# v through GpSimd's casting queue and two PE transposes, and w2 in 384 columns, in a linear-attention and soft-MoE kernel

## The chip, the cores and the metric

The kernel runs on one core of one Trainium2 chip. The metric is the time of one execution on the device, in microseconds. The kernel before took 122.52 us, the median of three runs (122.45 to 122.78). The engines are named as in the profile: PE (matrix multiply; PEld is its weight load), DVE (VectorE), ACT (ScalarE), POOL (GpSimd) and SP (a queue that only issues transfers). SP, ACT and POOL issue the transfers (DMAs), which 16 DMA engines carry out.

## What is computed

First a linear attention (RWKV-5): for each of 4 batches and 8 heads a state of 48 x 48 runs over 768 tokens. Then a soft mixture of experts over the resulting 3,072 tokens of 384 values: each of 32 slots is a weighted mean over all tokens, eight experts (two matrices each) handle four slots each, and every token takes a weighted mean of the slots.

```python
for t in range(S):                      # attention; B, H, S, D = 4, 8, 768, 48
    kt, vt, rt = (k[:, :, t], v[:, :, t], r[:, :, t])
    cur = np.einsum('bhd,bhe->bhde', u[None] * kt, vt)
    y[:, :, t] = np.einsum('bhd,bhde->bhe', rt, state + cur)
    state = w[None, :, :, None] * state + np.einsum('bhd,bhe->bhde', kt, vt)
...
logits = x @ phi                        # MoE; x is y as 3072 x 384, phi 384 x 32
slot_input = softmax(logits, 0).T @ x
for e in range(E):                      # 8 experts; w1 384 x 1024, w2 1024 x 384
    h = np.maximum(slot_input[e] @ w1[e], 0.0)
    slot_out[e] = h @ w2[e]
return softmax(logits, 1) @ slot_out
```

(The two softmax lines stand for their few lines of exp and division.)

## The kernel before

**Tiling.** Heads are worked on in pairs, so there are 16 units (4 batches x 4 pairs, index m), and each unit is cut into two halves of three 128-token chunks. That gives 32 iterations, i = 0 to 31, of the one loop at L494; it starts at i = -5 to fill the pipeline. In it mu = i // 2 and odd = i % 2. The order of the instructions on each engine is the order in which the program writes them.

**Inputs.** k, r and v of a batch lie in one of three buffers raw0 to raw2 (batch 3 takes raw0 again, once batch 0's has been used). A partition holds six consecutive tokens of k and r for each head (runs of 1,152 bytes), and three consecutive tokens of each half for v (runs of 576 bytes). SP issues all of these loads (L115, L119): batches 0 and 1 by pairs of heads, batch 2 whole, batch 3 at i = 3 (L552).

**One unit.** `scale` (L228, POOL, for unit 0 DVE) multiplies k and r by powers of the decay w and writes bf16 into kr. POOL does this three units ahead for k and two for r, one instruction an iteration. `t_pe` (L235) transposes on PE, `t_evac` (L241, ACT) copies the result to kT or rT and puts the tokens in order. `b_pe` and `b_evac` (L247, L252) transpose kT back by chunk to kn. For v, `v_cast` (L270, ACT; unit 0 on POOL, L268) makes bf16, and `v_pe` (L284) puts the tokens in order: for each chunk three matmuls with shifted columns of a selection matrix Q3 gather the three tokens of a partition into PSUM bank Vb, nine matmuls of 96 columns a half. `v_evac` (L290, ACT) copies them to vn. Then `a_pe` (L299) and `mask_f` (L304, DVE) form the masked scores, `m_pe` and `z_evac` (L325, L341, L342) the states, `y_pe` and `y_evac` (L352 to L372) the output.

**Start.** Before the loop DVE and ACT make the tables of decay powers W (`tt`, `ex`, L188, L192), from ln w, which `spread` (L177) broadcasts over the partitions with a ones matmul; the rest of the tables follow in the first iterations (T_AT). PE runs matmuls without use (`keep_warm`, L144) until there is work.

**Weights.** POOL issues the loads of w1 and w2 (L135, L138), which cast f32 to bf16 on the way, 768 KB written for each of 16 matrices. They stand in POOL's order at iterations 13 to 26 (W_AT, L465), one behind that iteration's scaling, up to five at i = 26, and the last w2 in three pieces after the loop (rows 0-4, 4-6 and 6-8 of eight, L576). Ahead of the first stands `guard` (L571), a copy of one column that waits until k of batch 3 has landed. w1 has its own buffer; w2 goes into raw1 and raw2 once batches 1 and 2 have been used. No more than eight of POOL's loads are outstanding: each waits for the eighth before it.

**After the loop** come the last routing steps, w1 (L623), the transposes of the hidden values (L648), w2 (`second`, L660; each row of four or fewer experts in two halves of 192 columns, into banks Xb and Yb), the scaling to so (L671, L672) and the output, 24 blocks of 128 tokens (`emit`, L684 to L688), stored by SP and POOL (L704).

Of the kernel before, what the change touches and what calls it, by code (L numbers as in the profile page):

```python
# [9 lines left out]
def kernel(  # L10
# [13 lines left out]
    B, H, S, D = r.shape  # L24
    C = 128
# [26 lines left out]
    def O(ins):  # L52
        return tc.keep_in_program_order(ins)
# [11 lines left out]
    EG = E // 2  # L65
    raw = [big.tile([128, 3 * RW], f32, name=f"raw{j}") for j in range(NR)]
    eW2 = nF * Dm
# [6 lines left out]
    def raw_of(which, b):  # L74
        return raw[b % NR][:, which * RW:(which + 1) * RW]

    T0 = psb.tile([128, 1024], bf, name="T0")
# [26 lines left out]
    O(dve.memset(wu[:], 1.0))  # L104
    O(sp.dma_start(out=w_row, in_=w.rearrange("(o h) d -> o (h d)", o=1)))
    O(act.preload_act_table_set("natural_log_exp_and_others"))
    O(act.dma_start(out=wu3[0:4, :, 0:D], in_=w.rearrange("(q e) d -> q e d", e=2)))
    O(act.dma_start(out=wu3[4:8, :, 0:D], in_=u.rearrange("(q e) d -> q e d", e=2)))
    O(dve.memset(warm, 0.0))
    O(dve.memset(one_f, 1.0))  # L110
    zt = cst.tile([128, nQ, 3, P2], f32, name="zt")
    O(dve.memset(zt[:], 0.0))

    def load_kr(which, src, b, h0, h1):
        O(sp.dma_start(out=raw_of(which, b).rearrange("p (h x) -> p h x", h=H)[:, h0:h1, :],  # L115
                       in_=src[b, h0:h1].rearrange("h (p j) d -> p h (j d)", j=J)))

    def load_v(b, h0, h1):
        O(sp.dma_start(out=raw_of(2, b).rearrange("p (h x) -> p h x", h=H * G)[:, h0 * G:h1 * G, :],  # L119
                       in_=v[b, h0:h1].rearrange("h (g p j) d -> p (h g) (j d)", g=G, j=JV)))  # L120

    def load_batch(b, step):
        for h0 in range(0, H, step):
            load_kr(0, k, b, h0, h0 + step)
            load_kr(1, r, b, h0, h0 + step)
            load_v(b, h0, h0 + step)

# [13 lines left out]
    def keep_warm(n, bank=Yb, data=None):  # L141
        data = warm if data is None else data
        for _ in range(n):
# [7 lines left out]
                         pattern=[[-1, 128]], channel_multiplier=1))  # L151
    QW = 2 * C + JV - 1 + C
    Q3 = cst.tile([128, QW], bf, name="Q3")
    O(pool.memset(Q3[:], 0.0))
    O(pool.affine_select(out=Q3[:], in_=Q3[:], compare_op=ALU.not_equal, fill=1.0, base=JV - 1,
                         pattern=[[-1, QW]], channel_multiplier=JV))
    mask_ut = cst.tile([128, 128], f32, name="mask_ut")
# [37 lines left out]
    tt(1, 0)  # L195
    spread(Vb, P2, H * D)
    ex(0, 0)
# [3 lines left out]
    def wu_steps(n):  # L201
# [5 lines left out]
        if n == 1:  # L207
            O(dve.tensor_mul(ucol[0:64, :, 0], wuT[0:64, 0:4], wuT[0:64, 4:8]))
            O(dve.tensor_mul(ucol[64:128, :, 1], wuT[64:128, 0:4], wuT[64:128, 4:8]))

    O(pool.memset(zt[0:64, :, :, 0:D], 1.0))
    O(pool.memset(zt[64:128, :, :, D:P2], 1.0))
    ones = cst.tile([128, 128], bf, name="ones")
    Le_t = [cst.tile([128, L, 128], bf, name=f"Le{j}") for j in range(2)]
    phi_s = cst.tile([128, nM, ES], bf, name="phi_s")
    phi_b = cst.tile([128, nM * ES], bf, name="phi_b")
    assert JV == nM
    acc = cst.tile([128, NA], f32, name="acc")
    guard = cst.tile([128, 1], f32, name="guard")
    st = {}  # L220
# [40 lines left out]

    def v_cast(m):
        b, q = divmod(m, nQ)
        vb = wk.tile([128, 2, G, JV, D], bf, name="v_bf", bufs=2)
        st["vb", m] = vb
        out, src = vb[:].rearrange("p h g j d -> p (h g j d)"), raw_of(2, b)[:, 2 * q * G * JV * D:2 * (q + 1) * G * JV * D]
        if m == 0:
            O(pool.tensor_copy(out, src))  # L268
        else:
            O(act.copy(out, src))  # L270


    def at(i):
        m, g = divmod(i, G)
        b, q = divmod(m, nQ)
        return m, b, q, g, b * G + g

    def v_pe(i):
        m, b, q, g, n = at(i)
        vb = st["vb", m]  # L280
        for c in range(L):
            for j in range(JV):
                o = C * c - j + JV - 1
                O(pe.matmul(Vb[:, c * P2:(c + 1) * P2], Q3[:, o:o + C], vb[:, :, g, j, :],  # L284
                            start=(j == 0), stop=(j == JV - 1)))

    def v_evac(i):
        vn = wk.tile([128, L, 2, D], bf, name="vn", bufs=3)
        st["v", i] = vn
        O(act.copy(vn[:].rearrange("p c e d -> p (c e d)"), Vb[:, 0:L * P2]))  # L290

# [145 lines left out]
    def route(i, part):  # L437
# [23 lines left out]
        if s < 2 * L:  # L461
# [4 lines left out]
    T_AT = {-4: [(tt, 0, 1), (tt, 1, 1), (ex, 0, 1), (tt, 0, 2)], -3: [(ex, 1, 1), (ex, 0, 2)],  # L466
            -1: [(tt, 1, 2), (ex, 1, 2)], 0: [(tt, 0, 3), (ex, 0, 3)], 1: [(tt, 1, 3), (ex, 1, 3)]}
    Z_AT = {-3: 0, -1: 1, 1: 2, 2: 3}
    nw = 0
# [24 lines left out]
    for i in range(-5, nH):  # L494
# [53 lines left out]
        if i == 2:  # L548
            O(pool.memset(ones[:], 1.0))
            for t in Le_t:  # L550
                O(pool.memset(t[:], 0.0))
        if i == 3:  # L552
            load_kr(0, k, B - 1, 0, H)
            load_kr(1, r, B - 1, 0, H)
            for h0 in range(0, H, 2):
                load_v(B - 1, h0, h0 + 2)
        if i == 5:
            O(act.copy(phi_b[:], phi_f))
        if i == 6:
# [10 lines left out]
        if i == min(W_AT):  # L570
            O(pool.tensor_copy(guard[:], raw_of(0, B - 1)[:, 0:1]))  # L571
# [81 lines left out]
    row_recip(0, 8)  # L653
    SO = [Xb[:, 0:HD], Yb[:, 0:HD]]

    def second(g, experts):
        for y in range(nF):
            for x in range(2):
                for j in experts:
                    O(pe.matmul(SO[x][32 * j:32 * j + 32, :], hT[g][:, y, 32 * j:32 * j + 32],  # L660
                                w2_of(g * EG + j)[:, y, x * HD:(x + 1) * HD],
                                start=(g == 0 and y == 0), stop=(g == 1 and y == nF - 1), skip_group_check=True))

# [5 lines left out]
    row_sums(8, 12)  # L669
    so = cst.tile([128, Dm], bf, name="so")  # L670
    O(dve.tensor_scalar_mul(so[:, 0:HD], SO[0], csr[:, 0:1]))  # L671
    O(act.activation(out=so[:, HD:Dm], in_=SO[1], func=AF.Copy, scale=csr[:, 0:1]))  # L672
    row_recip(8, 12)
# [3 lines left out]
    sizes = [1, 1, 2, 2, 2, 4, 4, 4, 4]  # L677
    obuf = ([raw[0][:, 16 * Dm:17 * Dm], raw[0][:, 17 * Dm:18 * Dm], Wf[0][:, 0:2 * Dm], Wf[1][:, 0:2 * Dm],
             Wf[0][:, 2 * Dm:4 * Dm]]
# [55 lines left out]
```

The softmax here doesn't subtract the row's maximum and nothing guards it: scores larger than these inputs give would overflow.

## Time and profile before

| | us |
|---|---|
| median of three runs | 122.52 |
| the profiled execution | 122.36 |
| its span, first to last instruction | 120.5 |
| busy: PE, DVE, ACT, POOL | 102.6, 96.4, 83.7, 59.7 |
| POOL's scalings, 30 x 1.426 | 42.2 |
| first issue of a weight load on POOL | 40.22 |
| last piece of w2 used by PE | 103.83 |

The span is what the trace shows from the first to the last instruction; the difference to the execution's time, 1.86 us, lies outside. A busy time is a sum of the durations of an engine's instructions; it says nothing yet of what the end waits for. The page also cuts the span into 40 slices of 3.01 us, with the busy share of each engine and of the DMA engines in tenths, and the chain of waits follows the end back through what released each step. A timeline gives one engine's instructions in order: start, duration, engine, line, operation, output and inputs, and in brackets the idle time ahead and what ended it.

### The profile page before, as it was taken

How to read it: one execution, taken by the hardware profiler on the slowest of the kernel's cores; microseconds unless marked ns; L12 is line 12 of the kernel's file. 1: busy time of each engine (PE TensorE's matmuls, PEld its weight loads, DVE VectorE, ACT ScalarE, POOL GpSimd, SP SyncE). 2: the span in 40 equal slices, each digit the busy share in tenths (PEclk: the TensorE clock that was granted, in tenths of full speed). 3: DMA queues.
4: the chain of work that ended last, by engine and by line, in shares of the span. 5: the costliest groups of instructions: out<-in, count | busy, mean ns of one | idle time of the engine just before them, and what ended most of it. 6: DMA issues, size and time to landing. Idle time of an engine off the chain costs nothing.

```text
span 120.5 us, 4334 instructions
## 1 busy us (share of the span) xinstructions
PE 102.6 (85%) x1795; PEld 82.9 (69%) x1797; DVE 96.4 (80%) x187; ACT 83.7 (69%) x183; POOL 59.7 (50%) x70
## 2 busy tenths in 40 slices
PE   5996977799999999999999999999979996796000
PEld 1465866687887988898888898888866686583000
DVE  6899999999999999899999899999943510399000
ACT  4459769797978998888898988997963510299000
POOL 7349534599999999797677593101000000012000
PEclk9999999999999999999999999999999999999755
DMA  2999999999999999999999999999999998069992
GB/s 38 322 362 373 374 367 371 364 391 362 330 380 382 323 204 216 218 213 212 220 206 222 211 220 209 215 215 215 224 208 220 208 206 165 16 261 389 396 420 100
DMA packets 20925, 31.79 MB, mean 264 GB/s; under 512 B 1129, under 2 KB 18026, under 8 KB 20906
## 3 DMA queue, kind: packets, MB, share of 16 engines
q0 software_dynamic: 2960, 14.55, 55.5%
q1 hardware_dynamic: 17922, 16.96, 41.3%
q8 instruction: 14, 0.23, 0.7%
q14 instruction: 5, 0.04, 0.1%
q10 hardware_dynamic: 24, 0.00, 0.0%
HBM read 39.38 MB, written 4.72 MB: 366 GB/s over the span
## 4 chain that ended last, share of the span: by engine, by line
PE 37%; DMA 31%; DVE 15%; issue 6%; ACT 1%; POOL 1%; POOLq 0%; DVEq 0%; ACTq 0%
DMA raw<-in_moe_w_dram 31%; PE Vb L284 5%; PE T L235 4%; PE Ab L299 4%; PE Yb L352 3%; DVE W L188 3%; PE T L247 2%; PE Mb L325 2%; DVE prod L257 2%; PE Yb L365 2%; DVE kn L252 2%; DVE Z L341 2%; PE Xb L387 2%; PE Xb L380 2%; PE Yb L144 2%
## 5 line engine op out<-in xcount | busy, mean ns | idle before, releaser
L228 POOL TENSOR_TENSOR kr<-raw,W 128x576 bf16<-128x576 f32 x30 | 42.2, 1426 | 12.4 <-PE T L235 5.2
L304 DVE TENSOR_TENSOR AT<-Ab,mask_ut 128x768 bf16<-128x768 f32 x32 | 30.2, 945 | 0.8 <-PE Ab L299 0.6
L284 PE MATMUL Vb<-v_bf,Q 128*128 128x96 bf16 x288 | 18.2, 211 | 0.0
L235 PE MATMUL T<-ident,kr 128*128 128x128 bf16 x192 | 17.2, 230 | 1.0 <-POOL kr L228 1.0
L284 PEld LDWEIGHTS <-Q 128*128 128x128 bf16 x288 | 16.3, 100 | 1.5 <-issue 0.2
L241 ACT COPY kT<-T 128x768 bf16<-128x768 bf16 x16 | 12.8, 799 | 4.6 <-PE T L235 3.3
L241 ACT COPY rT<-T 128x768 bf16<-128x768 bf16 x16 | 12.8, 800 | 4.2 <-PE T L235 3.6
L257 DVE TENSOR_TENSOR prod<-T,kT 128x768 bf16<-128x768 bf16 x16 | 15.2, 947 | 0.0
L342 DVE TENSOR_TENSOR dv<-vn,Mb 128x288 bf16<-128x288 bf16 x32 | 14.1, 440 | 0.0
L235 PEld LDWEIGHTS <-kr 128*128 128x128 bf16 x192 | 12.7, 102 | 1.8 <-POOL kr L228 1.2
L290 ACT CAST vn<-Vb 128x288 bf16<-128x288 f32 x32 | 13.4, 419 | 0.1
L372 ACT CAST x<-Yb 128x288 bf16<-128x288 f32 x32 | 13.1, 409 | 0.2 <-PE Yb L365 0.2
L341 DVE TENSOR_TENSOR Z<-Mb,zt 128x288 bf16<-128x288 f32 (+1 forms) x32 | 12.7, 395 | 0.6
L299 PE MATMUL Ab<-rT,kT 64*128 64x128 bf16 x192 | 11.1, 222 | 2.1 <-DVE AT L304 2.1
L704 POOL DMA_DIRECT2D out_dram<-W x1 | 0.5, 549 | 24.9 <-DVE W L686 24.9
L325 PE MATMUL Mb<-vn,kn 128*128 128x96 bf16 (+2 forms) x80 | 11.5, 242 | 0.0
L352 PE MATMUL Yb<-vn,AT 128*128 128x48 bf16 x192 | 10.3, 185 | 0.1
L270 ACT CAST v_bf<-raw 128x576 bf16<-128x576 f32 x15 | 10.2, 677 | 0.0
L299 PEld LDWEIGHTS <-kT 64*128 64x128 bf16 x192 | 5.6, 95 | 5.6 <-DVE AT L304 2.0
L138 POOL DMA_DIRECT2D raw<-in_moe_w_dram x10 | 5.5, 557 | 7.9 <-DMA raw<-in_moe_w_dram 6.5
L352 PEld LDWEIGHTS <-AT 128*128 128x128 bf16 x192 | 7.1, 96 | 3.3
L365 PE MATMUL Yb<-dv,ident 128*128 128x288 bf16 x32 | 9.1, 285 | 0.2
(143 smaller groups left out, 221.7 us busy)
## 6 DMA issues: line engine op xcount, KB each, us to landing
w_all<-in_moe_w_dram POOLq DMA_DIRECT2D x8, 768.0 KB, 12.7
raw<-in_moe_w_dram POOLq DMA_DIRECT2D x7, 768.0 KB, 18.4
raw<-in_v_dram SPq DMA_DIRECT2D x12, 288.0 KB, 6.2
raw<-in_k_dram SPq DMA_DIRECT2D x8, 288.0 KB, 6.1
raw<-in_r_dram SPq DMA_DIRECT2D x8, 288.0 KB, 5.9
raw<-in_k_dram SPq DMA_DIRECT2D x2, 1152.0 KB, 12.9
raw<-in_r_dram SPq DMA_DIRECT2D x2, 1152.0 KB, 10.3
out_dram<-raw POOLq DMA_DIRECT2D x2, 768.0 KB, 6.8
```

The source lines that it names most:

```text
L228: O(eng.tensor_mul(kr[:, j].rearrange("p j (h s) -> p j h s", s=64)[:, :, :, 0:D], src, W[j][:, q].rearrange("p j (h d) -> p j h d", h=2)))
L235: O(pe.transpose(bank[:, x * C:(x + 1) * C], kr[:, j, x, :], ident[:]))
L241: O(act.copy(t[:].rearrange("p (s j) -> p s j", j=J), bank[:, 0:S].rearrange("p (j s) -> p s j", j=J)))
L257: O(dve.tensor_mul(pr[:].rearrange("p (s j) -> p s j", j=J), T1[:, 0:S].rearrange("p (j s) -> p s j", j=J), st["kT", m][:].rearrange("p (s ...
L284: O(pe.matmul(Vb[:, c * P2:(c + 1) * P2], Q3[:, o:o + C], vb[:, :, g, j, :], start=(j == 0), stop=(j == JV - 1)))
L290: O(act.copy(vn[:].rearrange("p c e d -> p (c e d)"), Vb[:, 0:L * P2]))
L299: O(pe.matmul(Ab[:, e, c * C:(c + 1) * C], kT[s, t], rT[s, t]))
L304: O(dve.tensor_mul(AT[:], Ab[:, :, 0:T].rearrange("p e (c t) -> p e c t", c=L), mask_ut[:, None, None, :].to_broadcast([128, 2, L, C])))
L325: O(pe.matmul(o, kn[:, g * L + c, :], vc, start=first, stop=True, skip_group_check=True))
L341: O(dve.tensor_mul(Z[:], Mb[:, 0:x * P2].rearrange("p (c e) -> p c e", c=x), zt[:, q, 0:x, :]))
L342: O(dve.tensor_mul(dv[:], st["v", i][:].rearrange("p c e d -> p (c e) d"), Mb[:, 288:288 + 2 * L, None].to_broadcast([128, L * 2, D])))
L352: O(pe.matmul(Yb[:, o:o + D], AT[:, e, c, :], vn[:, c, e, :], start=first, stop=False, skip_group_check=True))
```

## The change

v of a batch is now read six tokens per partition, like k and r, by loads that POOL issues and that cast to bf16 (16 loads, one for each pair of heads). Batch 0's four are issued before the loop, between two memsets and the making of Q3, which moves behind the second of them; those of batches 1 to 3 at iterations 0 to 11, one an iteration (V_AT). v_cast goes. In even iterations PE transposes the pair's v, six transposes for each head of 48 rows (`vt_pe`), and ACT copies them with the tokens in order to vTs (`vt_evac`); in odd iterations six transposes turn that back by chunk (`vn_pe`) and one copy brings both halves of the unit to vn (`vn_evac`). DVE clears bank Vb once at the start, since 16 rows between the two heads are never written by the transposes.

Beside this: the row of w for `spread` is loaded on ACT's queue instead of SP's; the second spread uses bank Ab; batch 3's r comes in four pieces, and guard reads the second of them; the raw buffers are cut to 16 x 384 columns, with vTs (2 x 384) as a buffer of its own that also serves the first two output blocks; phi_b shares memory with acc, and so lies in a part of a W table that is free by then; `second` runs 384 columns at a time into one bank; the last w2 comes in rows 0-4, 4-7 and 7-8.

```diff
+    def v_of(b):
+        return raw[b % NR][:].bitcast(bf)[:, 2 * VO:2 * VO + RW].rearrange("p (h j d) -> p h j d", h=H, j=J)
...
-    O(sp.dma_start(out=w_row, in_=w.rearrange("(o h) d -> o (h d)", o=1)))
+    O(act.dma_start(out=w_row, in_=w.rearrange("(o h) d -> o (h d)", o=1)))
...
+    O(dve.memset(Vb[:], 0.0))
...
-    def load_v(b, h0, h1):
-        O(sp.dma_start(out=raw_of(2, b).rearrange("p (h x) -> p h x", h=H * G)[:, h0 * G:h1 * G, :],
-                       in_=v[b, h0:h1].rearrange("h (g p j) d -> p (h g) (j d)", g=G, j=JV)))
+    def load_v(b, q):
+        O(pool.dma_start(out=v_of(b)[:, 2 * q:2 * q + 2],
+                         in_=v[b, 2 * q:2 * q + 2].rearrange("h (p j) d -> p h j d", j=J)))
...
-    spread(Vb, P2, H * D)
+    spread(Ab[:, 0, :], P2, H * D)
...
+    load_v(0, 0)
     O(pool.memset(zt[0:64, :, :, 0:D], 1.0))
     O(pool.memset(zt[64:128, :, :, D:P2], 1.0))
+    load_v(0, 1)
+    QW = 2 * C + nM - 1 + C
+    Q3 = cst.tile([128, QW], bf, name="Q3")
+    O(pool.memset(Q3[:], 0.0))
+    O(pool.affine_select(out=Q3[:], in_=Q3[:], compare_op=ALU.not_equal, fill=1.0, base=nM - 1,
+                         pattern=[[-1, QW]], channel_multiplier=nM))
+    load_v(0, 2)
+    load_v(0, 3)
...
-    def v_cast(m):
...
+    Vh = Vb[:].bitcast(bf)
+    PV = 64 + D
+
+    def vt_pe(m):
         b, q = divmod(m, nQ)
+        vb = v_of(b)
+        for j in range(J):
+            for e in range(2):
+                O(pe.transpose(Vh[64 * e:64 * e + D, j * C:(j + 1) * C], vb[:, 2 * q + e, j, :], ident[:]))
+
+    def vt_evac(m):
+        vT = vTs[:].bitcast(bf)[0:PV, (m % 2) * S:(m % 2 + 1) * S]
+        st["vT", m] = vT
+        O(act.copy(vT.rearrange("p (s j) -> p s j", j=J),
+                   Vh[0:PV, 0:S].rearrange("p (j s) -> p s j", j=J)))
+
+    def vn_pe(m):
+        vT = st["vT", m]
+        for c in range(nC):
+            O(pe.transpose(Vh[:, c * C:c * C + PV], vT[:, c * C:(c + 1) * C], ident[0:PV, 0:PV]))
+
+    def vn_evac(m):
+        vn = wk.tile([128, nC, 2, D], bf, name="vn", bufs=3)
+        for g in range(G):
+            st["v", m * G + g] = vn[:, g * L:(g + 1) * L]
+        O(act.copy(vn[:].rearrange("p c e d -> p (c e) d"),
+                   Vh[:, 0:S].rearrange("p (x s) -> p x s", s=64)[:, :, 0:D]))
...
+    V_AT = {j: (1 + j // nQ, j % nQ) for j in range((B - 1) * nQ)}
...
-        if 0 <= i + 2 < nH:
-            v_pe(i + 2)
-            v_evac(i + 2)
+        if 0 <= mu + 2 < nU:
+            if odd:
+                vn_pe(mu + 2)
+                vn_evac(mu + 2)
+            else:
+                vt_pe(mu + 2)
+                vt_evac(mu + 2)
...
-        if odd == 0 and 0 <= mu + 2 < nU:
-            v_cast(mu + 2)
...
+        if i in V_AT:
+            load_v(*V_AT[i])
         if i == 3:
             load_kr(0, k, B - 1, 0, H)
-            load_kr(1, r, B - 1, 0, H)
             for h0 in range(0, H, 2):
-                load_v(B - 1, h0, h0 + 2)
+                load_kr(1, r, B - 1, h0, h0 + 2)
...
-            O(pool.tensor_copy(guard[:], raw_of(0, B - 1)[:, 0:1]))
+            O(pool.tensor_copy(guard[:], raw_of(1, B - 1)[:, 2 * J * D:2 * J * D + 1]))
...
-    for y0, y1 in ((0, 4), (4, 6), (6, 8)):
+    for y0, y1 in ((0, 4), (4, 7), (7, 8)):
         load_w(nw, y0, y1)
...
-    SO = [Xb[:, 0:HD], Yb[:, 0:HD]]
+    SO = Xb[:, 0:Dm]
 
     def second(g, experts):
         for y in range(nF):
-            for x in range(2):
-                for j in experts:
-                    O(pe.matmul(SO[x][32 * j:32 * j + 32, :], hT[g][:, y, 32 * j:32 * j + 32],
-                                w2_of(g * EG + j)[:, y, x * HD:(x + 1) * HD],
-                                start=(g == 0 and y == 0), stop=(g == 1 and y == nF - 1), skip_group_check=True))
+            for j in experts:
+                O(pe.matmul(SO[32 * j:32 * j + 32, :], hT[g][:, y, 32 * j:32 * j + 32],
+                            w2_of(g * EG + j)[:, y, :],
+                            start=(g == 0 and y == 0), stop=(g == 1 and y == nF - 1), skip_group_check=True))
```

More of the change, by code (lines that the diff above doesn't have):

```diff
@@ L65 @@
     EG = E // 2
-    raw = [big.tile([128, 3 * RW], f32, name=f"raw{j}") for j in range(NR)]
+    VO = 2 * RW
+    RT = 16 * Dm
+    raw = [big.tile([128, RT], f32, name=f"raw{j}") for j in range(NR)]
+    vTs = big.tile([128, 2 * Dm], f32, name="vTs")
     eW2 = nF * Dm
@@ L125, in load_batch @@
             load_kr(1, r, b, h0, h0 + step)
-            load_v(b, h0, h0 + step)
     load_batch(0, 2)
@@ L151 @@
                          pattern=[[-1, 128]], channel_multiplier=1))
[L152 to L156, printed above, removed]
     mask_ut = cst.tile([128, 128], f32, name="mask_ut")
@@ L215 @@
     phi_s = cst.tile([128, nM, ES], bf, name="phi_s")
-    phi_b = cst.tile([128, nM * ES], bf, name="phi_b")
-    assert JV == nM
     acc = cst.tile([128, NA], f32, name="acc")
+    phi_b = acc[:].bitcast(bf)[:, 0:nM * ES]
     guard = cst.tile([128, 1], f32, name="guard")
@@ L259, in prod_f @@
                          st["kT", m][:].rearrange("p (s j) -> p s j", j=J)))
-    def v_cast(m):
+    Vh = Vb[:].bitcast(bf)
+    PV = 64 + D
+    def vt_pe(m):
         b, q = divmod(m, nQ)
[L264 to L270, printed above, removed]
+        vb = v_of(b)
[17 more added lines that the diff above has]
+                   Vh[:, 0:S].rearrange("p (x s) -> p x s", s=64)[:, :, 0:D]))
     def at(i):
@@ L276, in at @@
         return m, b, q, g, b * G + g
[L278 to L290, printed above, removed]
     def a_pe(i):
@@ L551 @@
                 O(pool.memset(t[:], 0.0))
+        if i in V_AT:
+            load_v(*V_AT[i])
         if i == 3:
             load_kr(0, k, B - 1, 0, H)
-            load_kr(1, r, B - 1, 0, H)
             for h0 in range(0, H, 2):
-                load_v(B - 1, h0, h0 + 2)
+                load_kr(1, r, B - 1, h0, h0 + 2)
         if i == 5:
-            O(act.copy(phi_b[:], phi_f))
+            O(act.copy(phi_b, phi_f))
         if i == 6:
@@ L669 @@
     row_sums(8, 12)
-    so = cst.tile([128, Dm], bf, name="so")
-    O(dve.tensor_scalar_mul(so[:, 0:HD], SO[0], csr[:, 0:1]))
-    O(act.activation(out=so[:, HD:Dm], in_=SO[1], func=AF.Copy, scale=csr[:, 0:1]))
+    so = Wf[1].bitcast(bf)[:, 2 * F + nM * ES * 8:2 * F + nM * ES * 8 + Dm]
+    O(dve.tensor_scalar_mul(so[:, 0:HD], SO[:, 0:HD], csr[:, 0:1]))
+    O(act.activation(out=so[:, HD:Dm], in_=SO[:, HD:Dm], func=AF.Copy, scale=csr[:, 0:1]))
     row_recip(8, 12)
@@ L677 @@
     sizes = [1, 1, 2, 2, 2, 4, 4, 4, 4]
-    obuf = ([raw[0][:, 16 * Dm:17 * Dm], raw[0][:, 17 * Dm:18 * Dm], Wf[0][:, 0:2 * Dm], Wf[1][:, 0:2 * Dm],
+    obuf = ([vTs[:, 0:Dm], vTs[:, Dm:2 * Dm], Wf[0][:, 0:2 * Dm], Wf[1][:, 0:2 * Dm],
              Wf[0][:, 2 * Dm:4 * Dm]]
```

## The prediction

> **What bounds the kernel now.** I read the busy and DMA rows of the page first, then the chain of waits, then GpSimd's own order of time, and last the start-up. The profiled execution took 122.36 us with a span of 120.5 us, so 1.86 us lie outside the span.
>
> ```profile
> POOL 7349534599999999797677593101000000012000
> ...
> DMA  2999999999999999999999999999999998069992
> GB/s 38 322 362 373 374 367 371 364 391 362 330 380 382 323 204 216 218 213 212 220 206 222 211 220 209 215 215 215 224 208 220 208 206 165 16 261 389 396 420 100
> ```
>
> A slice is 3.01 us. The DMA engines are full from slice 2 to slice 33, that is from 3 to 102 us: first f32 inputs at about 370 GB/s (slices 2 to 14), then the weights, which are cast on the way, at about 215 GB/s written. Whatever PE and VectorE do in between, the last weight can't land before all this traffic has passed.
>
> ```profile
> 66.26 15.18 DMA raw<-in_moe_w_dram
> ...
> 81.97 21.82 DMA raw<-in_moe_w_dram
> ...
> 103.83 0.24 PE Xb L660
> ```
>
> In the chain of waits the last w2 piece is released at 81.97 and PE uses it at 103.83. The 21.82 us are no cost of that piece (192 KB): it stands in a queue that is always full. So the end is set by when the weight stream began.
>
> ```profile
> 24.33 0.78 POOL L551 MEMSET Le<- 128x384 bf16 x2
> 25.07 15.09 POOL L228 TENSOR_TENSOR kr<-raw,W 128x576 bf16<-128x576 f32 x11
> 40.09 0.20 POOL L571 COPY guard<-raw 128x1 f32<-128x1 f32 x1
> 40.22 0.75 POOL L135 DMA_DIRECT2D w_all<-in_moe_w_dram  x1
> 40.98 1.42 POOL L228 TENSOR_TENSOR kr<-raw,W 128x576 bf16<-128x576 f32 x1
> 42.35 0.59 POOL L135 DMA_DIRECT2D w_all<-in_moe_w_dram  x1
> ```
>
> GpSimd's timeline: from 25.07 it runs eleven scalings back to back, 1.37 us each, then the guard, then issues the first w1 at 40.22. Nothing it waits for stands between; the first weight is late only because GpSimd gets there then. An issue occupies it: 0.59 us, and the scaling behind begins after it. The other engines' loop takes about 2.3 us an iteration, so GpSimd at 1.37 us catches up here; that is the cover which the page's "50% busy" hides.
>
> ```profile
> 6.92 0.85 PE L235 MATMUL T<-ident,kr 128*128 128x128 bf16 x6
> ...
> 7.81 0.80 ACT L241 COPY kT<-T 128x768 bf16<-128x768 bf16 x1 [1.33 <-PE T L235]
> ...
> 9.84 0.54 DVE L252 COPY kn<-T 128x768 bf16<-128x768 bf16 x1
> ...
> 10.30 0.82 DVE L208 TENSOR_TENSOR ucol<-wuT 64x4 bf16<-64x4 f32 x1
> ```
>
> At the start VectorE runs without a gap from 5.94 us into the loop, and everything up to 25 us follows it.
>
> ```profile
> 98.93 0.25 PE L660 MATMUL Yb<-raw,W 128*32 128x192 bf16 x2
> ...
> 99.60 0.24 PE L660 MATMUL Xb<-raw,W 128*32 128x192 bf16 x1 [0.42 <-DMA raw<-in_moe_w_dram]
> ```
>
> After 99.0 us PE only follows the weights. It has 32 matmuls of 0.083 us left (2.65 us) and ends at 104.16, so its path has about 2.3 us of slack.
>
> **What the Trainium skill says.** "DMA: Bandwidth & Descriptors", SWDGE vs HWDGE vs iDMA: a cast in a DMA can be issued by GpSimd only, and its cores write the descriptors. The trace agrees that this is work on GpSimd (0.53 to 0.75 us an issue). The same page, Anatomy of one DMA: generation costs little and grows slowly with the number of descriptors; here 192 KB and 768 KB issues differ by 0.03 us, but all have 128 rows, while a v load has 256 runs. "TensorEngine Tiling (Array Packing)", Key Properties: tiles of the array work in parallel, and changing the mode drains it. The trace agrees for 32-column tiles (four L660 matmuls of 192 columns start every 0.083 us).
>
> **The change, part by part.**
>
> Inputs. SP loses 13 v loads (8,192 packets of 576 B) and reads k and r alone; v becomes 16 casting loads, 4,096 runs of 1,152 B read. Windows of 2 us show 392 GB/s from 24 to 28, while k and r of batch 2 pass (counted by bytes from the start), and 350 and 332 from 28 to 32, while its v does. At about 340, v costs 4.72/0.340 = 13.9 us of traffic now; at k's and r's 390 it would be 12.1: a gain of 1.8 us, if the traffic were still what decides. Bounds: 0 (casting runs no faster) and 2.9 (the weights' 430 GB/s read).
>
> GpSimd. Loads of batch 0 go out before the loop, those of batches 1 to 3 at iterations 0 to 11, each ahead of the next scaling. Q3's 0.93 us moves behind the second one and is needed only by iteration 6; the 1.21 us cast of pair 0 goes. Iterations 0 and 1 have cover (1.62 and 1.41 us idle before the scalings at 20.02 and 22.84). Iterations 2 to 11 have none: ten issues enter the run that starts at 25.07. Price of one: not below 0.53, the smallest issue; above, 256 runs instead of 128 may double it, 1.1. I take 0.62, as the rows show nearly no dependence on size: 10 x 0.62 = 6.2 us. What stands behind each is the next scaling, and PE's transposes wait for that; at 1.37 + 0.62 = 1.99 us an iteration GpSimd still keeps the loop's 2.3, so the loop hardly waits. The first w1, at iteration 13, waits for all ten.
>
> Start-up. PE must transpose v of pair 0 before k (12 transposes in front of L235's 6.92), and ScalarE copies it (0.80) before kT. v was issued at 2.10 and used at 7.34; now it leaves GpSimd at about 2 and shares the engines with k and r, so it lands at about 7, as PE ends its warming matmuls. 12 transposes at the start's slow rate (six took 0.85) cost 0.8 in pairs, 1.7 one by one. Then k's copy ends at 9.5 instead of 8.6; vn's six transposes (0.6) also precede b_pe, so kn moves from 9.84 to about 11.1. VectorE's new memset of Vb (0.5, scaled from zt's 1.02 for 1,152 elements) is inside that. The shift is 1.3 us; bounds 0.5 (PE in its fast rate) and 2.3 (v late, one by one). w_row on ScalarE's queue lets k start 0.4 us earlier, worth nothing here.
>
> So the first w1 goes out at 40.22 + 1.3 + 6.2 = 47.7.
>
> The weights. 16 x 768 KB = 12.58 MB at 216 GB/s take 58.2 us. They end at about 102.5 now (the windows 100:102 and 102:104 show 162 and 33 GB/s), so the stream stands as if begun at 44.3, 4.1 us after its first issue, because the rest of r and v passed with it. After the change k, r and v are through before (k and r of batch 3, issued at about 25.5, take 2.36/0.39 = 6 us and v's drip), so the engines stand nearly idle from some 34 to 48 us, and the stream begins about 1.5 us after the issue (estimate: SP's first k load, issued at 1.14, moved data from about 2.3, and GpSimd's issue is 0.3 longer). That gives 2.6 us back: 7.5 - 2.6 = 4.9 us later. The buffers of w2 are free long before, as batches 1 and 2 are used by iteration 18.
>
> The guard now reads the second of r's four pieces; at 46 us that has long landed. Cost nothing.
>
> PE in the loop. Nine Vb matmuls took 0.38 by the chain, 0.76 a pair. Six vn transposes cost 0.30 (0.34 for 128 columns, now 112), twelve vt ones 0.33 (two tiles at once) to 0.68 (serial): 0.63 to 0.98. I take 0.75, no change. ScalarE: 15 casts of 0.68 and 32 copies of 0.42 (23.6) become 16 of 0.80 and 16 of about 0.65 (scaled between 288 and 768 elements), 23.2: no change. Both hide under the weights, which leave PE 2.3 + 4.9 us less what the start-up took; without that cover the serial case costs 0.22 x 16 = 3.5.
>
> The end. 64 matmuls of 384 columns replace 128 of 192: same columns. After the last piece one matmul (0.16) instead of four (0.33): 0.2 gained. Longer gaps between weights could let PE slow down; 0 to 0.5, taken as 0. The moved buffers (vTs, so, phi_b, Ab for spread) add no wait that is late.
>
> Sum: 122.36 + 4.9 - 0.2 = 127.1 for a profiled execution; the median shown, 122.52, is 0.16 above it, so 127.2.
>
> **Rivals.**
>
> Faster: the start of the weights doesn't move, because issues overlap scalings or the start-up gains; then the stream begins at 41.7 instead of 44.3, and the time is 122.36 - 2.6 - 0.2 + 0.16 = 119.7. For it: 8,192 short packets are gone and GpSimd has half its time free on average. Against: the timeline shows issue and scaling strictly one after the other, and no free time from 25 to 40 us. It decides when the first w1 leaves before 42.8.
>
> No change: first w1 at about 42.8, which needs 0.13 us an issue with the start-up as worked out. 122.5. No row is that small.
>
> PE becomes the bound: serial transposes (3.5) and the start-up (1.3) make 4.8 against 2.3 of slack, +2.5 - 0.2: 124.8. For it: PE is at 99% from 24 to 85 us. Against: it shows only if the weights are not later still, which takes issues below about 0.4.
>
> A dear issue, 1.0 us, is the forecast's mechanism with its upper price: +3.8, 131.0.
>
> **How the numbers follow.** Forecast's mechanism 0.82 (of which a dear issue 0.12), PE bound 0.06, faster 0.08, no change 0.04. A measurement tells 0.3% from no change. Faster 0.08, same 0.04, slower 0.88. The forecast's own range with issues of 0.53 to 0.9 and a start-up of 0.5 to 2.3 is 125.4 to 130.6; 124.7 takes in the PE case, and 131.0 the dear issue.
>
> **What would show it.** Right: the first w1 issue near 47.7; v loads on GpSimd at about 0.6 us between scalings from 26 to 46 us; low digits in the DMA row from 34 to 48 us, then 9s at 215 GB/s to about 107; last L660 group released by a DMA near 108.7; kn's first copy near 11. Wrong: DMA full through 40 us; the first w1 at or before 42.8; PE without waits for w2 at the end; or a weight stream at another rate than 216 GB/s.

## The result, and the profile after

The changed kernel takes 131.59 us (median of 4, 131.05 to 132.18) against 122.65 before (122.45 to 122.83): a ratio of 1.073, 95% interval 1.068 to 1.078. It is 8.9 us slower, 4.4 more than predicted and 0.6 above the range. The profiled execution took 132.18 us, with a span of 130.4. Executions of one kernel can fall into a slower state; among all runs below only two of the combined kernel did, its profiled one among them, and its ratio leaves them out.

The page of the changed kernel: GpSimd's busy tenths, the DMA engines' busy tenths, and what they moved, in slices of 3.26 us.

```profile
POOL 6943727799999999999999933111000000012000
DMA  4999999999997573999999999999999999259990
GB/s 108 190 318 272 344 384 387 335 319 339 289 144 74 75 81 34 199 213 214 213 218 215 214 211 216 219 216 211 217 215 215 212 209 207 45 203 385 403 420 36
```

Before, the DMA row was full from slice 2 to slice 33 and the rate fell straight from some 380 to 215 GB/s. Now there is a hole between the inputs and the weights: four slices with 34 to 81 GB/s. The engines aren't idle in it, though: their busy tenths still read 7, 5, 7 and 3 there. The weights run at about the rate of before, 207 to 219 GB/s, only later. GpSimd's row reads 9 in every slice from 9 to 23.

GpSimd's timeline shows what makes the hole (start, duration, line, operation):

```profile
26.32 0.20 POOL L565 MEMSET ones<- 128x128 bf16 x1
26.47 0.77 POOL L567 MEMSET Le<- 128x384 bf16 x2
27.19 0.76 POOL L126 DMA_DIRECT2D raw<-in_v_dram  x1
27.98 1.42 POOL L237 TENSOR_TENSOR kr<-raw,W 128x576 bf16<-128x576 f32 x1
29.32 0.76 POOL L126 DMA_DIRECT2D raw<-in_v_dram  x1
...
46.46 0.76 POOL L126 DMA_DIRECT2D raw<-in_v_dram  x1
47.24 2.79 POOL L237 TENSOR_TENSOR kr<-raw,W 128x576 bf16<-128x576 f32 x2
49.97 0.18 POOL L588 COPY guard<-raw 128x1 f32<-128x1 f32 x1
50.09 0.61 POOL L141 DMA_DIRECT2D w_all<-in_moe_w_dram  x1
```

The eleven scalings that ran back to back now alternate with ten v issues. Each takes its 0.76 us out of GpSimd's time, and the first w1 leaves at 50.09 instead of 40.22.

The chain of waits (start, length, what) at both ends:

```profile
1.95 6.79 DMA raw<-in_v_dram
8.78 0.86 PE Vb L279 x12
...
87.19 25.02 DMA raw<-in_moe_w_dram
112.26 0.82 PE Xb L676 x4
```

Near its start stands the first v load, which PE waits for until 8.78; the chain ends as before with a w2 piece in a full queue, 8.4 us later (103.83 to 112.26).

Four marks cut the execution into terms that can be compared: GpSimd's memset of `ones` (it follows the start-up), the first w1 issue, the first matmul after the last wait for w2, and the end.

| profiled execution | memset of ones at | to the first w1 | to the last w2's use | to the end | time |
|---|---|---|---|---|---|
| before | 24.19 | 16.03 | 63.61 | 18.53 | 122.36 |
| after | 26.32 | 23.77 | 62.17 | 19.92 | 132.18 |
| difference | +2.13 | +7.74 | -1.44 | +1.39 | +9.82 |

The sum is exact. This execution is the slowest of its four, 0.59 above their median.

### The profile page after: what moved, and what is told of

It is laid out like the page before. It is cut to its first block, busy times and chain, and to the rows that moved or that the text cites. A ratio compares the mean times of both kernels' runs of the same rounds, so it can differ in the third digit from the quotient of the medians.

```text
span 130.4 us, 4162 instructions
## 1 busy us (share of the span) xinstructions
PE 103.8 (80%) x1733; PEld 77.9 (60%) x1733; DVE 94.7 (73%) x188; ACT 85.2 (65%) x168; POOL 70.1 (54%) x85
## 4 chain that ended last, share of the span: by engine, by line
DMA 38%; DVE 35%; issue 7%; PE 5%; ACT 5%; POOL 1%; POOLq 1%; DVEq 0%
DMA raw<-in_moe_w_dram 33%; DVE AT L317 11%; DVE prod L266 7%; DVE dv L355 6%; DMA raw<-in_v_dram 5%; DVE kn L261 4%; DVE Z L354 3%; DVE W L189 2%; ACT W L193 2%; DVE raw L702 1%; ACT vTs L284 1%; PE Vb L279 1%; PE Xb L676 1%; ACT rT L250 1%; ACT kT L250 1%
## 5 line engine op out<-in xcount | busy, mean ns | idle before, releaser
L244 PE MATMUL T<-ident,kr 128*128 128x128 bf16 x192 | 16.6, 225 | 0.3 <-DVE AT L317 0.2
L284 ACT COPY vTs<-Vb 112x768 bf16<-112x768 bf16 x16 | 13.0, 811 | 3.0 <-PE Vb L279 2.8
L676 PE MATMUL Xb<-raw,W 128*32 128x384 bf16 x64 | 7.8, 374 | 6.8 <-DMA raw<-in_moe_w_dram 6.8
L244 PEld LDWEIGHTS <-kr 128*128 128x128 bf16 x192 | 12.2, 100 | 0.9 <-POOL kr L237 0.5
L126 POOL DMA_DIRECT2D raw<-in_v_dram x16 | 12.2, 761 | 0.0
L296 ACT COPY vn<-Vb 128x576 bf16<-128x576 bf16 x16 | 10.7, 667 | 0.0
L279 PE MATMUL Vb<-ident,raw 128*48 128x128 bf16 x192 | 8.7, 229 | 1.8 <-DMA raw<-in_v_dram 1.6
## 6 DMA issues: line engine op xcount, KB each, us to landing
w_all<-in_moe_w_dram POOLq DMA_DIRECT2D x8, 768.0 KB, 12.7
```

Source lines behind the costliest of these rows:

```text
L126: O(pool.dma_start(out=v_of(b)[:, 2 * q:2 * q + 2], in_=v[b, 2 * q:2 * q + 2].rearrange("h (p j) d -> p h j d", j=J)))
L244: O(pe.transpose(bank[:, x * C:(x + 1) * C], kr[:, j, x, :], ident[:]))
L284: O(act.copy(vT.rearrange("p (s j) -> p s j", j=J), Vh[0:PV, 0:S].rearrange("p (j s) -> p s j", j=J)))
```

## The experiments

All durations below are of the one profiled execution of each kernel; times and ratios are of its runs beside the kernel before on the same chip. The runs of the changed kernels lie within 1.0 us of their median (once 1.6), those of the kernel before mostly within 0.5.

**Issues or traffic?** In the first kernel the twelve v loads of batches 1 to 3 are left out (every pair takes batch 0's v). The second keeps their issues, with the same 256 runs each but 32 bytes a run, into a place that nobody reads, and also takes batch 0's v everywhere.

```diff
-    V_AT = {j: (1 + j // nQ, j % nQ) for j in range((B - 1) * nQ)}
+    V_AT = {}
...
-        vb = v_of(b)
+        vb = v_of(0)
```

> The changed kernel without the twelve v loads of batches 1 to 3; their units use batch 0's v, so that the output of those batches isn't the reference's. Neither their issues on GpSimd nor their traffic are there. Theory I (issues on GpSimd hold back the first weight): ten issues of 0.78 us leave the run before it, so the first w1 goes out at about 50.1 - 7.8 = 42.3 us and the time falls by 7.8, to about 123.8. Theory T (the traffic of the casting runs holds the weights back): the first w1 may move, and the time falls too, to 124 or less, as 12 loads of some 1.35 us leave the engines. Theory S (start-up and the end of the kernel cost most): under 3 us gained, above 128.5.

```diff
+        dst, src = v_of(min(b, 1))[:, 2 * q:2 * q + 2], v[b, 2 * q:2 * q + 2].rearrange("h (p j) d -> p h j d", j=J)
+        if b:
+            dst, src = dst[:, :, 0, 0:16], src[:, :, 0, 0:16]
...
-        vb = v_of(b)
+        vb = v_of(0)
```

> The same with the twelve issues kept, but each of their 256 runs moves 16 elements instead of 288, into a place that nobody reads; v of batches 1 to 3 is left out as before. Issues stay, traffic nearly goes. Theory I: nothing gained over the changed kernel, first w1 at about 50 us, 130.5 to 131.6. Theory T: as without the loads, 124 to 125. Theory S: 131.

Without the issues: 123.86 us, ratio 1.014 (1.007 to 1.021), first w1 at 41.60. With the issues and nearly no bytes: 131.57, ratio 1.073 (1.067 to 1.080), first w1 at 50.12. That is the changed kernel's time to 0.02 us. The windows from 38 to 50 us (length, then busy time and count of PE, PEld, DVE, ACT and POOL, granted clock, DMA share, GB/s), first of the changed kernel, then of the second experiment:

```profile
38.00:50.00 12.00, 11.76 (x245) 9.92 (x241) 12.00 (x24) 11.20 (x23) 11.89 (x12) 1.00 0.65 75
```

```profile
38.00:50.00 12.00, 11.76 (x243) 9.92 (x242) 12.00 (x23) 11.21 (x23) 11.89 (x12) 1.00 0.19 6
```

The DMA engines go from 0.65 busy to 0.19 and 75 GB/s to 6, and no engine's work changes: v's traffic costs nothing there, GpSimd's time does. An issue takes 0.76 us in the second kernel too, so its price doesn't come from the bytes. The kernel without the issues also shows that PE doesn't bind: all its new transposes are in it, and it still waits for the last w2 piece (0.59 us, at 104.21).

**Weights earlier.** All the work is done, but the w1 and w2 loads are asked for from the seventh half step on, between the v issues.

```diff
-    W_AT = {13: 1, 14: 1, 15: 1, 16: 1, 18: 1, 19: 1, 20: 1, 22: 1, 23: 1, 25: 1, 26: 5}
+    W_AT = {7: 1, 8: 1, 9: 1, 11: 1, 13: 1, 14: 1, 16: 1, 18: 1, 20: 1, 22: 1, 24: 1, 26: 4}
```

> The changed kernel with the first w1 at iteration 7 instead of 13, the others spread behind it. All work is done. Theory I: first w1 at about 39 us, the half-empty stretch from 36 to 50 us fills; v loads behind it cost what their bytes cost at the weights' rate, 0.7 us each: last weight about 103.4, time about 122.7. Theory T: first w1 at 39 as well, but the five v loads still to pass cost 1.35 us each (their measured share, 0.65 of the engines in 2.14 us): last weight about 106.5, time about 126. Theory S: 128 or more.

124.61 us, ratio 1.017 (1.011 to 1.022); between the two expectations. The page's DMA row has no hole left:

```profile
DMA  3999999999997999999999999999999996089990
```

The first w1 leaves at 38.83. From the memset that is 11.3 us less than in the changed kernel, but from there to the last use of w2 it takes 65.72 instead of 62.17: 3.6 us are given back, in a stretch in which four v loads are issued behind the first weight and have to pass together with the weights. The end is 0.8 longer, because its last wait releases eight matmuls instead of four. The issues set the start of the stream; that v's traffic takes the 3.6 us once the engines are full fits the numbers, but no run tests it alone.

**The last step.** w2 in two halves of 192 columns and two banks, as before; nothing else.

```diff
-    SO = Xb[:, 0:Dm]
+    SO = [Xb[:, 0:HD], Yb[:, 0:HD]]
...
+            for x in range(2):
```

> The changed kernel with w2's products in two halves of 192 columns and two banks, as before. If the one bank makes ScalarE's half of so wait for VectorE's (113.56 after 113.11), 0.45 us come back: about 131.1. If the slow clock of PE at the end (half from 101 to 109 us) is what makes the end longer, nothing changes: 131.6, and the two halves of so start together while the first output matmul still comes more than 1.2 us after the last piece.

131.40 us, ratio 1.075 (1.069 to 1.080): by the median, undecided within the scatter. The timelines decide the mechanism. The changed kernel, then this one:

```profile
112.26 0.81 PE L676 MATMUL Xb<-raw,W 128*32 128x384 bf16 x4 [0.60 <-DMA raw<-in_moe_w_dram]
...
113.11 0.42 DVE L687 TENSOR_SCALAR W<-Xb,csr 128x192 bf16<-128x192 f32 x1 [14.46 <-PE Xb L676]
...
113.56 0.42 ACT L688 ACTIVATE W<-Xb,csr 128x192 bf16<-128x192 f32 x1 [15.09 <-DVE W L687]
...
114.03 0.24 PE L700 MATMUL T<-W,LexpT 128*128 128x192 bf16 x1 [0.21 <-ACT W L688]
...
114.76 0.83 SPq L720 DMA_DIRECT2D out_dram<-vTs  x2
```

```profile
112.19 0.42 DVE L688 TENSOR_SCALAR W<-Xb,csr 128x192 bf16<-128x192 f32 x1 [14.30 <-PE Xb L677]
112.27 0.42 ACT L689 ACTIVATE W<-Yb,csr 128x192 bf16<-128x192 f32 x1 [14.56 <-PE Yb L677]
...
113.47 0.83 SPq L721 DMA_DIRECT2D out_dram<-vTs  x2
```

With one accumulator of 384 columns, both halves of the experts' output are read from the one bank Xb, and ScalarE waits for VectorE; with two banks they start 0.08 us apart. The Trainium skill, "PSUM — Partial Sum Buffer", section "PSUM bank collisions raise a hardware error", says why a program orders them: the hardware doesn't arbitrate between two engines on one bank, and two reads count as a collision. The trace agrees as far as the order goes. From the first matmul after the last wait for w2 (111.40 here) to the first store of the output this kernel took 2.07 us against 2.50. The gain of 0.43 is clear of the scatter: in five other kernels with one bank this stretch is 2.50 or 2.51, wherever the last wait releases four matmuls. The time to the end, 19.45 against 19.92, doesn't show it, as the kernel without v loads needs 19.47 with one bank.

**The start.** The first v load is moved ahead of GpSimd's iota and masks.

```diff
+    load_v(0, 0)
     s_i = cst.tile([128, J], i32, name="s_i")
...
-    load_v(0, 0)
     O(pool.memset(zt[0:64, :, :, 0:D], 1.0))
```

> The first v load is issued as GpSimd's first instruction of the body, ahead of the iota, the two masks and their memsets (so at about 0.85 us instead of 1.95), everything else as in the changed kernel. Theory S (start-up: the late landing of the first v load, 8.74 us, holds TensorE and with it every step up to the memsets of GpSimd at 26.3): v lands 0.5 to 1.1 earlier, the first v transposes start at 7.8 or before, TensorE's wait for that load is below 0.7 us, GpSimd's first counted issue moves from 27.19 to about 26.3, the first w1 issue from 50.09 to about 49.2, the time from 131.6 to about 130.7. Rival S2 (the start is set by other things by then, the first k, r and weight steps or TensorE's clock): v lands earlier, but the first counted issue stays within 0.3 of 27.2 and the time within the spread of 131.6.

131.19 us, ratio 1.072 (1.069 to 1.075). PE's first v transposes, the changed kernel's and then this one's:

```profile
8.78 0.84 PE L279 MATMUL Vb<-ident,raw 128*48 128x128 bf16 x12 [1.65 <-DMA raw<-in_v_dram]
```

```profile
7.55 0.84 PE L279 MATMUL Vb<-ident,raw 128*48 128x128 bf16 x12 [0.42 <-DMA raw<-in_v_dram]
```

They start 1.23 earlier, and the first issue between the scalings (27.19 to 25.96) and the first w1 (50.09 to 48.86) move by exactly as much; the time by 0.4 in the medians, 1.2 in the profiled executions. The table over all experiments below says more: with the load in its old place PE starts on v anywhere from 7.33 to 8.78, and in six of the eight kernels the memset of `ones` follows 17.5 us after that start. In the other two (starts at 7.78 and 7.85) it comes a microsecond later. So in six of eight Theory S fits (the landing of the first v sets the start-up), but the earlier issue itself is worth less than the scatter of that landing.

**What an issue costs.** v of batches 1 to 3 in loads of four heads, and of eight.

```diff
-    V_AT = {j: (1 + j // nQ, j % nQ) for j in range((B - 1) * nQ)}
+    V_AT = {2 * j: (1 + j // 2, j % 2, H // 2) for j in range((B - 1) * 2)}
```

> v of batches 1 to 3 comes in six loads of four heads (512 runs each) instead of twelve of two heads (256 runs), one after every second half step; batch 0 as in the changed kernel. Theory N (an issue costs by its runs: 0.60 us at 128 runs and 0.76 at 256, so 0.44 + 1.25 ns a run): one costs 1.08 us, the five after the 27 us mark 5.4 instead of ten for 7.8, the first w1 issue is at about 47.7, the time about 129.2. Rival C (an issue costs about the same whatever its runs, and 128 against 256 differ for another reason): one costs 0.76 us, five 3.8, first w1 at about 46.1, time about 127.6. Rival R (cost in proportion to the runs): one costs 1.5 us, first w1 at 50.1, time unchanged at 131.6.

127.60 us, ratio 1.043 (1.039 to 1.047), first w1 at 44.93. GpSimd's timeline:

```profile
24.82 0.21 POOL L565 MEMSET ones<- 128x128 bf16 x1
...
25.69 0.81 POOL L126 DMA_DIRECT2D raw<-in_v_dram  x1
26.51 2.78 POOL L237 TENSOR_TENSOR kr<-raw,W 128x576 bf16<-128x576 f32 x2
...
44.93 0.61 POOL L141 DMA_DIRECT2D w_all<-in_moe_w_dram  x1
```

An issue of 512 runs costs 0.81 us where one of 256 costs 0.76. Rivals N (1.08) and R (1.5) fall; C is right on the price within 0.05 us (its first w1 was put too late because the start-up took 0.6 us here, not 2.1; that its time of 127.6 was met is luck, as the stream behind took 0.7 us longer, 62.83 instead of 62.17). With half the issues 4.0 us of the loss are gone by the medians; of the 4.8 between the profiled executions 3.7 lie between the memset and the first w1, and 1.5 in the earlier start-up.

```diff
-    V_AT = {j: (1 + j // nQ, j % nQ) for j in range((B - 1) * nQ)}
+    V_AT = {4 * j: (1 + j, 0, H) for j in range(B - 1)}
```

> v of batches 1 to 3 comes in one load of eight heads each (1,024 runs), after half steps 0, 4 and 8; batch 0 and all else as in the changed kernel. The first of the three lies in GpSimd's slack before 25 us, the other two between the back-to-back scalings. Theory I (what the changed kernel loses is the number of issues between the scalings, at some 0.8 us each however many runs one has): one issue costs 0.85 to 0.95, two 1.8, the first w1 issue is at 40.22 + 1.8 + 0.6 to 2.1 (start-up, by when the first v lands) = 42.6 to 44.1, the time 124.8 to 126.2. Theory T (the casting traffic of v itself): the same bytes in the same runs are moved, so where it begins to bind, the guard waits for the last r load and the first w1 issue is not before 46, the time 128 or more. Rival R (an issue's price grows with its runs from here on): one costs 1.5 or more, first w1 at 44 to 45.5, time 126 to 127.5.

128.56 us, ratio 1.047 (1.041 to 1.053): outside Theory I's 124.8 to 126.2, with the first w1 at 45.63. An issue of 1,024 runs costs 0.94 to 0.95, as I said, but PE's timeline has a new wait:

```profile
31.84 0.84 PE L279 MATMUL Vb<-ident,raw 128*48 128x128 bf16 x12 [4.26 <-DMA raw<-in_v_dram]
```

The first of the big loads is issued at 19.56 and lands 12.2 us later as a whole, while PE needs its first two heads at 27.6. Theory T would have shown in a guard that waits for r; it waited for nothing. The transposes came late instead: GpSimd waits before each of the three scalings from 39 to 45 us, twice for PE's transposes, 2.2 us in all, and the first w1 comes 2.3 later after the memset than two issues alone would put it (20.22 instead of 16.03 + 1.9). One load's latency took the place of the issues saved.

The table of terms for these kernels:

| profiled execution | v transposes start | memset of ones at | to the first w1 | to the last w2's use | to the end | time |
|---|---|---|---|---|---|---|
| after | 8.78 | 26.32 | 23.77 | 62.17 | 19.92 | 132.18 |
| no v loads in the loop | 8.07 | 25.58 | 16.02 | 62.61 | 19.47 | 123.68 |
| issues, few bytes | 7.78 | 26.39 | 23.73 | 62.02 | 19.92 | 132.06 |
| weights early | 7.85 | 26.38 | 12.45 | 65.72 | 20.68 | 125.23 |
| w2 in two banks | 8.02 | 25.55 | 23.72 | 62.13 | 19.45 | 130.85 |
| first v load first | 7.55 | 25.10 | 23.76 | 62.14 | 19.95 | 130.95 |
| v by four heads | 7.33 | 24.82 | 20.11 | 62.83 | 19.65 | 127.41 |
| v by batch | 7.89 | 25.41 | 20.22 | 63.15 | 19.56 | 128.34 |

**Versions to beat the kernel before.** First all of it together: four-head loads in the first half steps, the weights from the seventh on, two banks, the first v load first.

> The changed kernel with four things put together: v of batches 1 to 3 in six loads of four heads in the first half steps, the weights asked for from the seventh half step on (one at a time between the scalings), w2 in two halves of 192 columns, and the first v load as GpSimd's first instruction. Theory: the weights' stream begins as early as with early weights alone (first w1 at about 38) and the last piece is used at about 104, the halves of the experts' output run together (-0.45), the start-up gives up to 0.9: 123.4, between 122.9 and 124.3; still not below the kernel before, because the casting v loads keep the DMA engines about 7 us longer than before's v did, of which the hole between the loads and the weights gives back most. Rival: the engines are the bound from 4 us to the end and the early start of single parts gives nothing: 124.6.

Ratio 1.009 (1.005 to 1.012), that is 1.1 us above before, 123.7, within the theory's 122.9 to 124.3. These four things together bring the loss from 7.3% to 0.9%; what each of them gives in the combination isn't shown. Then the kernel before with the two small edits of the change that touch neither v nor GpSimd, and each of the two alone:

```diff
-    O(sp.dma_start(out=w_row, in_=w.rearrange("(o h) d -> o (h d)", o=1)))
+    O(act.dma_start(out=w_row, in_=w.rearrange("(o h) d -> o (h d)", o=1)))
...
-    for y0, y1 in ((0, 4), (4, 6), (6, 8)):
+    for y0, y1 in ((0, 4), (4, 7), (7, 8)):
```

> The kernel before with only the two small edits that touch neither v nor GpSimd: the row of w is loaded through ScalarE's queue, so that SyncE's first k load is issued 0.4 us earlier, and the last expert's w2 comes in pieces of four, three and one instead of four, two and two. Theory: the loads of k, r and v are what the DMA engines do up to 40 us, and start 0.2 to 0.4 earlier; the last piece's matmuls are half as many, 0.1 to 0.2 less after it lands. Together 0.2 to 0.6 faster than before: about 122.2. Rival: the first w1 issue (40.22) is set by GpSimd's scalings, which wait for the weights' exponentials, not for k, and the end does not move: 122.6, no difference.

> The kernel before with one edit alone: the row of w is loaded through ScalarE's queue. In the run with both small edits the last wait of TensorE for w2 released eight matmuls at once (103.78) where before it released four (103.83), so the piece of one was not there before the piece of three, and the end was 0.28 later from the last landing to the output of the experts (104.56 less 103.78, against 104.28 less 103.83 = 0.45). Theory: without the other split the gain at the start stays and that 0.3 comes on top: 121.8, a ratio to before of about 0.994. Rival: the whole gain of the two edits (0.5) came from the split or is no gain of the start: 122.6, ratio 1.000.

> The kernel before with the last expert's w2 in pieces of four, three and one instead of four, two and two, and nothing else. The row of w alone gave no difference (ratio 0.9996), both edits together 0.9972. Theory: the split alone carries it, the time is 122.3 or less and the ratio 0.997. Rival: neither edit alone gives anything, the two together do, or the 0.28% was chance: ratio 0.999 to 1.001.

| kernel before with | median | ratio to before (95%) |
|---|---|---|
| both edits | 122.07 | 0.9972 (0.9955 to 0.9989) |
| the row of w through ScalarE's queue | 122.62 | 0.9996 (0.9984 to 1.0008) |
| pieces of four, three, one | 122.49 | 0.9984 (0.9970 to 0.9998) |

Both edits together beat both kernels, by 0.3% over the kernel before, small, but with an interval that excludes no change. The row alone gives nothing, though k does start earlier (the first SP issue of k at 0.73 instead of 1.14); my theory for it fell, as in the run with both edits the first w1 stayed at 40.24. The split alone gives 0.16%, barely clear of no change. That the last landing released eight matmuls instead of four in one profiled execution made me expect a loss from it. The stretch from that wait to the first store is indeed longer (2.06 after 1.73), but the time shows no loss. Why the two add up to more than their parts is open; the difference of 0.1% may be chance.

## Why the prediction was wrong

The direction, the mechanism and the place were right: ten issues between scalings that have no cover, the first w1 late by their sum, a drop in the GB/s row before it, and the end following the stream. The sum missed because four terms were all off to the same side (profiled executions, us; the one of the changed kernel was its slowest, so by the medians the miss is 4.4):

| term | predicted | measured | off by |
|---|---|---|---|
| start-up | +1.3 | +2.13 | 0.8 |
| ten issues on GpSimd | +6.2 | +7.74 | 1.5 |
| the stream begins sooner after the first issue | -2.6 | -1.44 | 1.2 |
| the end | -0.2 | +1.39 | 1.6 |
| sum | +4.7 | +9.82 | 5.1 |

*Issue price.* The step "I take 0.62, as the rows show nearly no dependence on size" failed. All of GpSimd's weight issues in the profile before had 128 rows, and the first of them (40.22) did take 0.75; a v load has 256 runs, as the prediction itself said. The value was 0.77 with the gap, inside the bounds of 0.53 and 1.1, yet taken near the lower one. Doubling and redoubling the runs then adds only 0.05 and 0.14 us. That agrees with the page cited in the prediction ("DMA: Bandwidth & Descriptors", Anatomy of one DMA: the cost grows slowly with the descriptors). So the first doubling, from the weights' 128 runs and 0.60 to 256 and 0.76, costs more than the second; whether that is the runs or something else in the form of a v load was not tried.

*Start-up.* The step that v "lands at about 7" held only roughly. The law of the table (memset 17.5 us after PE's start on v) puts the predicted 1.3 at a start of 7.96; the starts of the seven kernels with the load in its old place average 7.96. Such a start is a landing 0.9 later than "about 7", so the sum of the step was nearer than its parts, by luck. The mean shift of the seven is 1.6, and the profiled execution of the changed kernel had the latest v of them. The two kernels that miss the law by a microsecond, weights early and issues with few bytes, ran PE at a slow rate again: six transposes at 15.6 us took 0.80 in both, 0.49 in the kernel without v loads. In weights early the windows 14:16 and 16:18 show the granted clock at 0.67 and 0.50; in the other the clock row reads 1.00, and why PE was slow stays open.

*Stream.* The step "the stream begins about 1.5 us after the issue" failed. By the prediction's own measure (the last use less 1.3 us, less 58.2 us at 216 GB/s, is 52.8) it was 2.7. In the kernel without v issues, where the engines stood idle before, the first bytes moved in the window 42.8 to 43.4, 1.2 us after the issue at 41.60, but until 44.6 the engines wrote only 92 to 154 GB/s, and 205 from there. What I left out fits this: one load alone does not fill the engines, and the second comes 2 us later (43.59), behind a scaling. The v loads that were still to land are not the reason: with nearly no bytes in them this term is the same (62.02 against 62.17).

*End.* "After the last piece one matmul (0.16) instead of four (0.33): 0.2 gained" failed twice over. One wait releases four matmuls of 384 columns (112.26 in the timeline above), because the piece of one does not come after the piece of three. And "the moved buffers (…, so, …) add no wait that is late" overlooked that SO itself went from two banks to one. Before, both halves were read side by side:

```profile
103.83 0.24 PE L660 MATMUL Xb<-raw,W 128*32 128x192 bf16 x1 [0.41 <-DMA raw<-in_moe_w_dram]
...
104.28 0.42 DVE L671 TENSOR_SCALAR so<-Xb,csr 128x192 bf16<-128x192 f32 x1 [7.27 <-PE Xb L660]
104.36 0.42 ACT L672 ACTIVATE so<-Yb,csr 128x192 bf16<-128x192 f32 x1 [7.53 <-PE Yb L660]
...
105.56 0.84 SPq L704 DMA_DIRECT2D out_dram<-raw  x2
```

From the first matmul after that wait to the first store it was 1.73 us before and is 2.50 now. With two banks and the new pieces it is 2.07 (w2 in two banks; 2.06 in the kernel before with both edits, further up), so 0.34 of the 0.77 belong to the pieces and 0.43 to the bank. The stores then take as long as before: 12.7 us from the first issue to the last byte, in both. Another 0.7 lies behind them: the windows 118.2:118.4 (before) and 127.4:127.6 (changed) show the last data, and the spans end at 120.5 and 130.4, so 2.2 and 2.9 us pass in which no engine works and no data moves. In the other kernels of the changed family this rest is 2.4 to 3.0; why is open. With 0.08 less outside the span, 0.77 and 0.70 make the 1.39.

*PE and the inputs.* No change for PE was right: in the chain of the kernel without v loads the twelve transposes of a pair take 0.45 us and the six of the way back 0.30, together the 0.75 that was taken. The gain that v's traffic was bounded with, 0 to 2.9 us, had the wrong sign: the casting loads are slower. In the window 38 to 50 us six of them fill 0.65 of the engines, 1.3 us of all engines each, so 16 take about 21 us by this estimate where v took some 13.9 before by the prediction's. So the engines did not stand "nearly idle" before the first w1, as the prediction had it, though that cost the changed kernel nothing.

The rival "faster" asked for a first w1 before 42.8, and with the start-up as it was (26.32 + 16.03 = 42.35) not one issue of v fits between the scalings. "PE becomes the bound" is refuted by the kernel without issues. The "dear issue" was the nearest. The range failed for another reason than the price: the issues and the start-up stayed inside the bounds that it gave them (0.77 and 2.13), and alone would have made 129.6. But the stream's 1.5 us and the end's 0.2 had no bounds that entered it, and these two terms hold 2.8 of the 5.1 us. (By its own terms the range for issues of 0.53 to 0.9 and a start-up of 0.5 to 2.3 ends at 131.0, not 130.6.)

## What to carry to other kernels

Count what an engine has to issue before the transfer that sets the end: each casting load on GpSimd cost it 0.53 to 0.95 us of its own time here, growing far slower than its size, so few large loads are cheaper than many small ones, up to the size where the first consumer waits for a whole load. When terms of a sum are estimates from neighbouring rows, give each of them a bound, the small ones and the gains too, and let the range follow their sum. When an accumulator is merged into one bank, look at who reads it next: the two engines that read its halves side by side before became a queue here.

## What was not expected of the hardware

- Issue time on GpSimd: 0.60 us at 128 runs (weights), 0.76 at 256, 0.81 at 512, 0.95 at 1,024 (v). The first issue that GpSimd makes is dearer: 0.75 against 0.59 for the next one of the same kind before, 0.87 against 0.73 in the changed kernel.
- Casting loads with runs of 1,152 bytes read and 576 written: 0.65 of the DMA engines for 75 GB/s written, where the weights fill them at 215.
- TensorE's clock fell to half between w2 pieces: in the changed kernel PE had no matmul from 99.5 to 101.67 us, and the windows 101.4:101.6 and 101.8:102.0 show the granted clock at 1.00 and 0.50. "TensorE: Matmul & The Clock Gate", "What's actually happening", puts the fall after an idle window of about 3.4 us; here 2.2 us without work were enough. The clock had recovered by 109 us and cost the end nothing. In weights early it stood at 0.50 from 15 to 18 us, in the stretch where the start-up lost its microsecond.
